# A mixer-and-MLP kernel: the last x load split in two, one DMA transpose of normed tiles done on TensorE, w2's loads side by side

## The chip, the cores and the metric

The kernel runs on one core of one Trainium2 chip. The metric is the device time of one execution in microseconds (us). Before the change the median of three runs is 139.93 us (139.67 to 140.01).

## What is computed

x has 2048 rows of 512; all tensors are bf16. In short:

```python
B, S, D, F = 1, 2048, 512, 1792
h = gelu(layernorm(x) @ w1)                  # w1: 512 x 512
c = D // 4                                   # four groups of 128 columns, shifted along the rows
g0 = h[..., 0*c:1*c] shifted down by 1 row   # zeros come in at the ends
g1 = h[..., 1*c:2*c] shifted up by 1 row
g2 = h[..., 2*c:3*c] shifted down by 2 rows
g3 = h[..., 3*c:   ] shifted up by 2 rows
x1 = x + concat(g0, g1, g2, g3) @ w2         # w2: 512 x 512
out = x1 + gelu(layernorm(x1) @ w3) @ w4     # w3: 512 x 1792, w4: 1792 x 512
```

The layer norm has no gain or bias, and the Gelu is the tanh form.

## The kernel before

**Tiles.** The 2048 rows are 16 tiles of 128. Row `16 p + t` is partition `p` of tile `t`, so a shift by one row is a step from tile `t` to tile `t-1` or `t+1` in the same partition, and only the first and last tiles need a step of one partition. A matmul that wants the 512 features on the partitions needs the tile transposed: four blocks of 128 by 128.

**Two ways through the first layer.** Tiles 0 to 5 are transposed raw by TensorE (`tp0` to `tp5`, line 351) into PSUM banks 6 and 7, copied to `xnT` by ScalarE (`ev`, line 360), multiplied by w1 (`m1r`, line 399), copied out (`rc`, line 409), and the normalisation is made good afterwards on VectorE and ScalarE (`zr`, `g1r`, and a DMA transpose `th_`). Tiles 6 to 15 go in pairs: VectorE takes the statistics (`st0_t`, `ag0_t`, lines 285 and 290), GpSimd the root of two tiles at once (`rs0_t`, line 296), VectorE writes the normed tile into `xn` (`nm0_t`, line 305), one DMA transposes the pair from `xn` to `xnT` (`td0_t`, line 371), TensorE makes h transposed for the pair (`m1p`, line 431: 16 matmuls of 128 by 256), and ScalarE takes the Gelu into `hTf` (`g1p`, line 441, or one tile at a time for tiles 10 and 11, `g1s`, line 446).

**After it.** `m2_t` (lines 457 and 472) multiplies the shifted windows of `hTf` by w2; tiles 8 and 9 are split, so that three of the four products of `m2_8` and two of `m2_9` (`m2_8a`, `m2_9a`) are ahead of those that need tiles 10 and 11. VectorE adds x (`x1_t`, line 482) and makes the second layer norm (`st1`, `ag1`, `nm1`), a DMA transposes the pair (`td1_t`, line 371), and TensorE does the MLP: `m3h` and `m3` (lines 514, 490), Gelu, `m4` (line 533), and VectorE's last add (line 545), with the output DMAs.

**Order.** Each engine runs its operations in an order written out by hand (`firsts`); what is not named follows in the order of the program. The wait of every operation is worked out from what it reads and writes, and an engine, or the DMA queue of SyncE (SP), stands at a waiting operation until it is released: what is queued behind it waits too. SP issues nearly all DMAs, loads and transposes alike, so a transpose that waits for its normed pair also holds the loads behind it, and the other way round. Around the change the order is:

- SP: the x tiles one by one (`ldx6` ... `ldx5`), `ldx12` for tiles 12 to 15 in one DMA, then `td0_6 td0_8 ldw20 td0_10 ldw21 ldw22 ldw23 td0_12 td0_14 ldw3a0 ldw3a1 th_0 ...`
- TensorE: `... tp5 m1r4 cs m1r5 m1p6 m1p8 m1p10 m2_8a m2_9a m2_8 m2_9 m1p12 m1p14 m2_10 ...`
- ScalarE: `... rc5 cse g1p6 g1p8 g1s10 g1s11 g1r0 g1r1 g1p12 g1p14 ...`
- VectorE: `... st0_10 st0_11 nm0_8 nm0_9 ag0_10 ag0_11 st0_12 st0_13 nm0_10 nm0_11 ag0_12 ag0_13 st0_14 st0_15 nm0_12 nm0_13 ag0_14 ag0_15 st0_1 ag0_0 ag0_1 nm0_14 nm0_15 zr0 zr1 st0_2 st0_3 ag0_2 ag0_3 x1_8 x1_9 ...`

The helper `tp(t, n, b, raw)` can transpose `n` tiles into one bank and can read `xn` in place of `x_sb`; before the change it is only called with one raw tile.

Of the kernel before, what the change touches and what calls it, by code (L numbers as in the profile page):

```python
# [26 lines left out]
class Program:  # L27
# [7 lines left out]
    def add(self, eng, name, fn, reads=(), writes=(), dma=False):  # L35
        self.ops.append(Op(name, eng, fn, reads, writes, dma))
# [129 lines left out]
def bass_standalone__mixer_s_mlp__prompt_kernel(nc: bass.Bass, x, w1, w2, w3, w4, out):  # L166
# [15 lines left out]
    with ExitStack() as es:  # L182
# [63 lines left out]
        def bres(b, n, tag):  # L246
            return [(("ps", b + i), tag) for i in range(n)]
# [19 lines left out]
        def load_x(t, n, eng="sp"):  # L267
            add(eng, f"ldx{t}", lambda e: e.dma_start(x_sb[:, t : t + n, :], xd[:, t : t + n, :]),  # L268
                writes=[(("x", i), 0) for i in range(t, t + n)], dma=True)
# [9 lines left out]
        def dst_of(layer, t):  # L279
            return (xn, t, ("xn", t), 0) if layer == 0 else (x1n, POS[t] % 8, ("x1n", POS[t] % 8), t)  # L280
# [61 lines left out]
        def tp(t, n, b, raw):  # L342
            src = x_sb if raw else xn
            rd = [(("x", i), 0) if raw else (("xn", i), 0) for i in range(t, t + n)]

            def f(e):
                ins = None
                for i in range(n):
                    for c in range(DC):
                        o = 1024 * b + (i * DC + c) * P  # L350
                        ins = e.transpose(psb[:, o : o + P], src[:, t + i, P * c : P * (c + 1)], ident[:])  # L351
                return ins

            add("pe", f"tp{t}", f, reads=rd + [("ident", 1)], writes=bres(b, 1, f"tp{t}"))

        def ev(t, n, b, eng="act"):
            src = psb[:, 1024 * b : 1024 * b + n * D]
            dst = xnT[:, t : t + n, :, :].rearrange("p t c s -> p (t c s)")
            if eng == "act":
                f = lambda e: e.activation(dst, src, ACT_F.Copy)  # L360
            else:
                f = lambda e: e.tensor_copy(dst, src)
            add(eng, f"ev{t}", f, reads=bres(b, 1, f"tp{t}"), writes=[(("xT", i), 0) for i in range(t, t + n)])


        def tdma(layer, t, n):
            dst = xnT if layer == 0 else x1nT
            src, k = dst_of(layer, t)[:2]
            p0 = t if layer == 0 else POS[t]
            add("sp", f"td{layer}_{t}",  # L370
                lambda e: e.dma_start(dst[:, p0 : p0 + n, :, :].rearrange("p t c s -> p (t c) s"),
                                      src[:, k : k + n, :].rearrange("p t d -> p (t d)"), transpose=True),
                reads=[dst_of(layer, i)[2:] for i in range(t, t + n)],
                writes=[(("xT", i) if layer == 0 else ("x1T", i), 0) for i in range(t, t + n)], dma=True)
# [205 lines left out]
        load_w1(2, "act")  # L580
        load_w1(3, "sp")
        load_x(1, 1, "act")
        for t, n in ((6, 1), (7, 1), (2, 1), (8, 1), (9, 1), (3, 1), (10, 1), (4, 1), (11, 1), (5, 1), (12, 4)):
            load_x(t, n)
        for c in range(DC):
            load_w2(c)
# [25 lines left out]
            else:  # L612
                norm(0, t)
        for t in range(R, NT, 2):
            tdma(0, t, 2)
        for t, b in ((6, 2), (8, 4), (10, 0), (12, 2), (14, 4)):
            m1p(t, b)
            if t == 10:
# [26 lines left out]
        for t in (8, 10):  # L645
# [8 lines left out]

        firsts = {}
        firsts["pe"] = """wu tp0 cs0 cs1 m1r01 m1r02 tp1 m1r03 m1r0 cs2 m1r12 tp2 m1r1 tp3 m1r2 tp4 m1r3 tp5 m1r4 cs m1r5 m1p6
            m1p8 m1p10 m2_8a m2_9a m2_8 m2_9 m1p12 m1p14 m2_10 m2_11 m2_12 m2_13 m2_14 m2_15""".split()
        firsts["act"] = """ldw10 ldw12 ldx1 table ev0 ev1 ev2 rc0 ev3 rc1 ev4 rc2 ev5 rc3 rc4 rc5 cse g1p6 g1p8 g1s10 g1s11
            g1r0 g1r1 g1p12 g1p14 g2h_0_0_0 g2h_0_0_4 g1r2 g1r3 g2h_0_0_8 g2h_0_0_12 g1r4 g1r5""".split()
        firsts["dve"] = """pada padb padc padd pade padf st0_0 st0_6 st0_7 ag0_6 ag0_7  # L660
            st0_8 st0_9 nm0_6 nm0_7 ag0_8 ag0_9 st0_10 st0_11 nm0_8 nm0_9 ag0_10 ag0_11
# [4 lines left out]
            st1_12 st1_13 ag1_12 ag1_13""".split()  # L666
        firsts["pool"] = """ident0 ident1 neghalf stz ste rs0_6 rs0_8 rs0_10
            rs0_12 rs0_14 rs0_0 rs0_2 rs1_8 rs1_10""".split()
        firsts["sp"] = """ldx0 ldw11 ldw13 ldx6 ldx7 ldx2 ldx8 ldx9 ldx3 ldx10 ldx4 ldx11 ldx5 ldx12 td0_6 td0_8 ldw20 td0_10 ldw21 ldw22 ldw23 td0_12 td0_14
            ldw3a0 ldw3a1 th_0 ldw3a2 ldw3a3 td1_8 ldw3b0 ldw3b1 ldw3b2 ldw3b3 td1_10 th_2 th_4 td1_12 td1_14 ldw4""".split()  # L670

        slots = [4, 0, 2]
# [110 lines left out]
```

## Time and profile before

| | |
|---|---|
| runs | 139.67, 139.93, 140.01 us |
| the profiled execution | 139.81 us, of which its span (first to last instruction) 137.9 |
| granted TensorE clock | 1.000 |
| TensorE busy (matmul) | 131.8 us, 96% of the span |
| VectorE, ScalarE, GpSimd busy | 57.9, 45.6, 12.4 us |
| DMA | 13.23 MB in 25336 packets, of which 17776 under 512 B |

How to read it: the views are of one profiled execution, with times in us from the start of its span. PE is TensorE's matmuls, PEld its weight loads, DVE is VectorE, ACT ScalarE, POOL GpSimd, SP SyncE, and a name with a q is an engine's queue that issues DMAs. A timeline row has the start, the duration, the engine, the line, what is written and read, how many instructions it merges, and in brackets the idle time before it with what ended it. A row of DMA issues ends with the size and the time from issue to landing. The chain is the work that ended last, followed back from the end.

### The profile page before, as it was taken

How to read it: one execution, taken by the hardware profiler on the slowest of the kernel's cores; microseconds unless marked ns; L12 is line 12 of the kernel's file. 1: busy time of each engine (PE TensorE's matmuls, PEld its weight loads, DVE VectorE, ACT ScalarE, POOL GpSimd, SP SyncE). 2: the span in 40 equal slices, each digit the busy share in tenths (PEclk: the TensorE clock that was granted, in tenths of full speed). 3: DMA queues.
4: the chain of work that ended last, by engine and by line, in shares of the span. 5: the costliest groups of instructions: out<-in, count | busy, mean ns of one | idle time of the engine just before them, and what ended most of it. 6: DMA issues, size and time to landing. Idle time of an engine off the chain costs nothing.

```text
span 137.9 us, 1822 instructions
## 1 busy us (share of the span) xinstructions
PE 131.8 (96%) x721; PEld 68.2 (49%) x721; DVE 57.9 (42%) x135; ACT 45.6 (33%) x56; POOL 12.4 (9%) x25
## 2 busy tenths in 40 slices
PE   7897949999999999999999999999999999999993
PEld 2343846748887334444444444444444444444452
DVE  0496995589974787772223000022300002232222
ACT  3478326502896005553000455400045540000000
POOL 2042322220322002222000000000000000000000
DMA  4989979997047792445311100011110001111121
GB/s 115 321 265 212 80 183 234 245 220 186 5 90 138 176 363 70 81 80 103 85 38 38 38 0 5 0 38 38 38 38 0 5 0 38 38 38 38 38 72 47
DMA packets 25336, 13.23 MB, mean 96 GB/s; under 512 B 17776, under 2 KB 24688, under 8 KB 25328
## 3 DMA queue, kind: packets, MB, share of 16 engines
q1 hardware_dynamic: 24752, 12.69, 38.3%
q10 hardware_dynamic: 576, 0.43, 1.2%
q8 instruction: 6, 0.10, 0.3%
q14 instruction: 2, 0.02, 0.0%
HBM read 6.82 MB, written 2.10 MB: 65 GB/s over the span
## 4 chain that ended last, share of the span: by engine, by line
PE 85%; DMA 7%; SPq 4%; DVE 1%; issue 1%
PE ps L533 35%; PE ps L490 26%; PE ps L457 9%; PE ps L514 9%; DMA x_sb<-in_x_dram 4%; PE ps L431 4%; SPq L268 3%; DMA xnT<-xn 3%; PE ps L472 1%; SPq L564 1%; DVE st L285 1%; DVE xn L305 0%; DVE o_sb L545 0%; DVE mv L290 0%
## 5 line engine op out<-in xcount | busy, mean ns | idle before, releaser
L533 PE MATMUL ps<-w_sb,h2T 128*128 128x512 bf16 (+2 forms) x238 | 48.9, 366 | 0.0
L501 ACT ACTIVATE h2T<-ps 128x1024 bf16<-128x1024 f32 x21 | 21.5, 1024 | 46.5 <-PE ps L490 46.5
L545 DVE TENSOR_TENSOR o_sb<-ps,x_sb 128x512 bf16<-128x512 f32 (+2 forms) x17 | 11.2, 660 | 60.9 <-PE ps L533 60.9
L490 PE MATMUL ps<-x1nT,w_sb 128*128 128x512 bf16 x168 | 36.8, 379 | 0.0
L533 PEld LDWEIGHTS ps<-w_sb,h2T 128*128 128x128 bf16 x238 | 22.8, 98 | 25.9
L490 PEld LDWEIGHTS ps<-x1nT,w_sb 128*128 128x128 bf16 x168 | 16.4, 98 | 19.9
L285 DVE BATCH_NORM_STATS2 st<-x_sb 128x6 f32<-128x512 bf16 x32 | 20.4, 678 | 5.2 <-DMA x_sb<-in_x_dram 5.2
L296 POOL TENSOR_TENSOR rstd<-mv,neghalf 128x2 f32<-128x2 f32 x16 | 11.5, 720 | 49.8 <-DVE mv L290 49.6
L457 PE MATMUL ps<-w_sb,hTf 128*128 128x512 bf16 x56 | 12.7, 380 | 0.0
L482 DVE TENSOR_TENSOR x_sb<-ps,x_sb 128x512 bf16<-128x512 f32 x16 | 10.7, 687 | 4.7 <-PE ps L457 3.1
L514 PE MATMUL ps<-x1nT,w_sb 128*128 128x256 bf16 x112 | 12.4, 273 | 0.0
L514 PEld LDWEIGHTS ps<-x1nT,w_sb 128*128 128x128 bf16 x112 | 11.0, 98 | 1.5
L431 PE MATMUL ps<-xnT,w_sb 128*128 128x256 bf16 x80 | 9.2, 273 | 2.6 <-DMA xnT<-xn 2.6
L431 PEld LDWEIGHTS ps<-xnT,w_sb 128*128 128x128 bf16 x80 | 7.6, 98 | 4.4 <-DMA xnT<-xn 3.3
L525 ACT ACTIVATE h2T<-ps 128x1024 bf16<-128x1024 f32 (+1 forms) x8 | 7.1, 915 | 7.7 <-PE ps L514 7.7
L305 DVE TENSOR_SCALAR x1n<-x_sb,mv,rstd 128x512 bf16<-128x512 bf16 x16 | 5.9, 410 | 6.4 <-POOL rstd L296 6.4
L457 PEld LDWEIGHTS ps<-w_sb,hTf 128*128 128x128 bf16 x56 | 5.0, 98 | 7.0 <-DVE x_sb L482 2.2
L399 PE MATMUL ps<-w_sb,xnT 128*128 128x512 bf16 x24 | 6.8, 380 | 0.2
L441 ACT ACTIVATE hTf<-ps 128x1024 bf16<-128x1024 f32 x4 | 4.1, 1024 | 4.3 <-PE ps L431 4.3
L290 DVE BATCH_NORM_AGGREGATE mv<-st 128x2 f32<-128x9 f32 x32 | 4.8, 183 | 0.0
L360 ACT ACTIVATE xnT<-ps 128x512 bf16<-128x512 bf16 x6 | 3.6, 599 | 3.0 <-PE ps L351 3.0
L414 DVE SCALAR_TENSOR_TENSOR zraw<-ncs,mv,yraw 128x512 f32<-128x512 f32 x6 | 4.2, 743 | 0.0
(26 smaller groups left out, 30.5 us busy)
## 6 DMA issues: line engine op xcount, KB each, us to landing
out_dram<-o_sb SPq DMA_DIRECT2D x15, 128.0 KB, 1.8
w_sb<-in_w_dram SPq DMA_DIRECT2D x1, 1792.0 KB, 8.2
x_sb<-in_x_dram SPq DMA_DIRECT2D x11, 128.0 KB, 3.6
w_sb<-in_w_dram SPq DMA_DIRECT2D x4, 256.0 KB, 3.2
w_sb<-in_w_dram SPq DMA_DIRECT2D x6, 128.0 KB, 3.2
w_sb<-in_w_dram SPq DMA_DIRECT2D x4, 192.0 KB, 3.3
x_sb<-in_x_dram SPq DMA_DIRECT2D x1, 512.0 KB, 5.5
w_sb<-in_w_dram ACTq DMA_DIRECT2D x2, 128.0 KB, 3.5
```

The source lines that it names most:

```text
L285: add("dve", f"st{layer}_{t}", lambda e: e.bn_stats(st9[:, i, 0:6], src[:, t, :]), reads=[(r, 0)], writes=[(("st6", i), 0)])
L296: lambda e: e.tensor_tensor(rstd[:, i : i + n], mv[:, i : i + n, 1], neghalf[:, 0:n], ALU.pow),
L399: ins = e.matmul(bank(b), xnT[:, t, c, :], w1_sb[:, c, :], start=(c == 0), stop=(c == DC - 1))
L431: ins = e.matmul(dst, w1_sb[:, c, P * fc : P * (fc + 1)], xnT[:, t : t + 2, c, :], start=(c == 0), stop=(c == DC - 1))
L457: ins = e.matmul(bank(b), hTf[:, c0 : c0 + P], w2_sb[:, j, :], start=(j == 0), stop=(j == DC - 1))
L482: lambda e: e.tensor_tensor(x1_sb[:, t, :], bank(b), x_sb[:, t, :], ALU.add),
L490: ins = e.matmul(bank(b), w3_sb[:, c, P * fc : P * (fc + 1)], x1nT[:, 4 * q : 4 * q + 4, c, :], start=(c == 0), stop=(c == DC - 1))
L501: lambda e: e.activation(h2T[:, fc : fc + 2, q % 2, :], src, ACT_F.Gelu_apprx_tanh),
L514: ins = e.matmul(dst, w3_sb[:, c, P * (fc + i) : P * (fc + i + 1)], x1nT[:, t : t + 2, c, :], start=(c == 0), stop=(c == DC - 1))
L525: lambda e: e.activation(h2T[:, fc : fc + n, q % 2, 256 * k : 256 * (k + 1)], src, ACT_F.Gelu_apprx_tanh),
L533: ins = e.matmul(ps[:, 512 * b : 512 * b + c1 - c0], h2T[:, fc, q % 2, P * i : P * (i + 1)], w4_sb[:, fc, c0:c1], start=(fc == 0), stop=(f ...
L545: lambda e: e.tensor_tensor(o_sb[:, k % 4, c0:c1], ps[:, 512 * b : 512 * b + c1 - c0], x1_sb[:, t, c0:c1], ALU.add),
```

## The change

Three things are changed:

1. x tiles 12 to 15 are loaded by two DMAs of two tiles each, `ldx12` in the old place and `ldx14` on SP behind the first DMA transpose, `td0_6`.
2. The normed pair 10 and 11 is no longer transposed by a DMA. TensorE does eight transposes (`tp10`) from `xn` into bank 7 behind `m1p6`, and ScalarE copies them to `xnT` (`ev10`, 128 by 1024) ahead of `g1p6`.
3. The four loads of w2 are issued one after the other behind `td0_8`; `td0_10` no longer stands between the first and the second.

```diff
-        for t, n in ((6, 1), ..., (5, 1), (12, 4)):
+        for t, n in ((6, 1), ..., (5, 1), (12, 2), (14, 2)):
             load_x(t, n)
...
         for t in range(R, NT, 2):
-            tdma(0, t, 2)
+            if t == 10:
+                tp(t, 2, 7, False)
+                ev(t, 2, 7)
+            else:
+                tdma(0, t, 2)
...
         firsts["pe"] = """wu tp0 cs0 cs1 m1r01 m1r02 tp1 m1r03 m1r0 cs2 m1r12 tp2 m1r1 tp3 m1r2 tp4 m1r3 tp5 m1r4 cs m1r5 m1p6
-            m1p8 m1p10 m2_8a m2_9a m2_8 m2_9 m1p12 m1p14 m2_10 m2_11 m2_12 m2_13 m2_14 m2_15""".split()
-        firsts["act"] = """ldw10 ldw12 ldx1 table ev0 ev1 ev2 rc0 ev3 rc1 ev4 rc2 ev5 rc3 rc4 rc5 cse g1p6 g1p8 g1s10 g1s11
+            tp10 m1p8 m1p10 m2_8a m2_9a m2_8 m2_9 m1p12 m1p14 m2_10 m2_11 m2_12 m2_13 m2_14 m2_15""".split()
+        firsts["act"] = """ldw10 ldw12 ldx1 table ev0 ev1 ev2 rc0 ev3 rc1 ev4 rc2 ev5 rc3 rc4 rc5 cse ev10 g1p6 g1p8 g1s10 g1s11
...
-        firsts["sp"] = """ldx0 ldw11 ... ldx5 ldx12 td0_6 td0_8 ldw20 td0_10 ldw21 ldw22 ldw23 td0_12 td0_14
+        firsts["sp"] = """ldx0 ldw11 ... ldx5 ldx12 td0_6 ldx14 td0_8 ldw20 ldw21 ldw22 ldw23 td0_12 td0_14
             ldw3a0 ldw3a1 th_0 ldw3a2 ldw3a3 td1_8 ldw3b0 ldw3b1 ldw3b2 ldw3b3 td1_10 th_2 th_4 td1_12 td1_14 ldw4""".split()
```

More of the change, by code (lines that the diff above doesn't have):

```diff
@@ L582, in bass_standalone__mixer_s_mlp__prompt_kernel @@
         load_x(1, 1, "act")
-        for t, n in ((6, 1), (7, 1), (2, 1), (8, 1), (9, 1), (3, 1), (10, 1), (4, 1), (11, 1), (5, 1), (12, 4)):
+        for t, n in ((6, 1), (7, 1), (2, 1), (8, 1), (9, 1), (3, 1), (10, 1), (4, 1), (11, 1), (5, 1), (12, 2), (14, 2)):
             load_x(t, n)
@@ L668, in bass_standalone__mixer_s_mlp__prompt_kernel @@
             rs0_12 rs0_14 rs0_0 rs0_2 rs1_8 rs1_10""".split()
-        firsts["sp"] = """ldx0 ldw11 ldw13 ldx6 ldx7 ldx2 ldx8 ldx9 ldx3 ldx10 ldx4 ldx11 ldx5 ldx12 td0_6 td0_8 ldw20 td0_10 ldw21 ldw22 ldw23 td0_12 td0_14
+        firsts["sp"] = """ldx0 ldw11 ldw13 ldx6 ldx7 ldx2 ldx8 ldx9 ldx3 ldx10 ldx4 ldx11 ldx5 ldx12 td0_6 ldx14 td0_8 ldw20 ldw21 ldw22 ldw23 td0_12 td0_14
             ldw3a0 ldw3a1 th_0 ldw3a2 ldw3a3 td1_8 ldw3b0 ldw3b1 ldw3b2 ldw3b3 td1_10 th_2 th_4 td1_12 td1_14 ldw4""".split()
```

## The prediction

> **What bounds the kernel now.** I read the page first, then the chain that ended last in order of time, then TensorE's timeline around the only waits that the chain shows.
>
> ```profile
> span 137.9 us, 1822 instructions
> ...
> PE 85%; DMA 7%; SPq 4%; DVE 1%; issue 1%
> ...
> L431 PE MATMUL ps<-xnT,w_sb 128*128 128x256 bf16 x80 | 9.2, 273 | 2.6 <-DMA xnT<-xn 2.6
> ...
> L399 PE MATMUL ps<-w_sb,xnT 128*128 128x512 bf16 x24 | 6.8, 380 | 0.2
> ...
> L360 ACT ACTIVATE xnT<-ps 128x512 bf16<-128x512 bf16 x6 | 3.6, 599 | 3.0 <-PE ps L351 3.0
> ```
>
> ```profile
> 6.40 0.43 SPq L268
> ...
> 6.87 5.51 DMA x_sb<-in_x_dram
> ...
> 14.36 4.66 DMA xnT<-xn
> ...
> 19.06 1.92 PE ps L431 x16
> ...
> 111.36 24.22 PE ps L533 x126
> ```
>
> TensorE is 85% of the chain. The one large thing on the chain that is not TensorE is x tiles 12-15 (one load, 6.87 to 12.38), VectorE behind it, and the third DMA transpose (td0_10, 14.36 to 19.01). From 19.06 to the end the chain is TensorE alone, so any time by which m1p10 starts sooner shortens the kernel one for one, until another wait appears. TensorE's timeline gives the two waits and the pitch of everything around them:
>
> ```profile
> 10.50 0.39 PE L351 MATMUL ps<-ident,x_sb 128*128 128x128 bf16 x4
> 10.73 1.03 PE L399 MATMUL ps<-w_sb,xnT 128*128 128x512 bf16 x4
> ...
> 11.81 1.03 PE L399 MATMUL ps<-w_sb,xnT 128*128 128x512 bf16 x4
> 13.55 3.67 PE L431 MATMUL ps<-xnT,w_sb 128*128 128x256 bf16 x32 [0.72 <-DMA xnT<-xn]
> 19.06 1.92 PE L431 MATMUL ps<-xnT,w_sb 128*128 128x256 bf16 x16 [1.84 <-DMA xnT<-xn]
> 20.82 2.02 PE L472 MATMUL ps<-w_sb,hTf 128*128 128x512 bf16 x8
> ```
>
> Ends are modelled and overlap, so I count starts. m1r5 is the four at 11.81; they take 1.03 and one takes 0.38, a pitch of (1.03-0.38)/3 = 0.217, so m1p6 could start at 12.68 and starts at 13.55: 0.87 lost. m1p6 and m1p8 are 32 at (3.67-0.27)/31 = 0.110; m1p10 could start at 17.06 and starts at 19.06: 2.00 lost. The whole stake is 2.87 us.
>
> **The landings behind these waits.** From issue to landing, one row for each transfer:
>
> ```profile
> x_sb<-in_x_dram SPq DMA_DIRECT2D x1, 128.0 KB, 4.0
> xnT<-xn SPq DMA_TRANSPOSE x1, 4.3
> xnT<-xn SPq DMA_TRANSPOSE x1, 3.8
> w_sb<-in_w_dram SPq DMA_DIRECT2D x1, 128.0 KB, 3.0
> w_sb<-in_w_dram SPq DMA_DIRECT2D x1, 256.0 KB, 3.2
> x1nT<-x1n SPq DMA_TRANSPOSE x1, 3.0
> x1nT<-x1n SPq DMA_TRANSPOSE x1, 4.9
> ```
>
> In this order: ldx5, td0_6, td0_12, ldw23, ldw3a0, td1_10 (nothing else moving), td1_0. SP's timeline has their issues:
>
> ```profile
> 9.22 3.21 SPq L371 DMA_TRANSPOSE xnT<-xn  x2
> 11.20 1.23 SPq L371 DMA_TRANSPOSE xnT<-xn  x1
> 15.65 2.87 SPq L568 DMA_DIRECT2D w_sb<-in_w_dram  x3
> 18.56 2.62 SPq L371 DMA_TRANSPOSE xnT<-xn  x2
> 54.73 4.28 SPq L371 DMA_TRANSPOSE x1nT<-x1n  x2
> ```
>
> ldx5, issued just ahead of ldx12 at 6.40, lands at 10.4; ldx12 1.98 later. td0_6 is issued at 9.22 and lands at 13.52, 1.14 behind ldx12: it queues behind the load. td0_10 needs 4.66 where a transpose with nothing beside it needs 3.0. What hit it is in the queues of two short windows, 15.56 to 15.58 and 57.40 to 57.43:
>
> ```profile
> q8 instruction: 1, 0.02, 508.8%
> q8 instruction: 1, 0.02, 183.1%
> ```
>
> Each is one 16 KB instruction fetch that starts there. The first lies on td0_10, the second on td1_0 (54.73+4.9 = 59.6, 1.9 late). A fetch lengthens a transpose in flight by 1.7 to 1.9 us. Here the Trainium skill (Runtime: NRT & Kernel Launch, Instruction fetch mechanics) says that crossing such a boundary is mostly hidden; this trace disagrees, with 4.66 against 3.0, and by the page's word the two rivals with a fetch below would have no chance.
>
> **The change, part by part.**
>
> *x in two loads.* ldx12 carries 256 KB in place of 512. Half of 1.98 behind ldx5 is 11.4 (bounds: 10.4 were it free, 12.38 were the bytes not what counts; the halving is the nearest reading as the loads ahead move at about the same rate). td0_6 follows 1.14 later: 12.54; its floor is 9.22+3.0 = 12.2. That is before 12.68, so m1p6's wait goes: **gain 0.87**. ldx14 passes td0_6 on SP and so waits for nm0_7 with it; it is issued at about 10.5, holds SP 0.43, and is done before td0_8's own wait ends at 11.20. Its landing behind a transpose is bounded by ldw3a0, the same size: 3.2 after issue, 13.7. VectorE:
>
> ```profile
> 11.08 0.26 DVE L290 BATCH_NORM_AGGREGATE mv<-st 128x2 f32<-128x9 f32 x2
> 12.40 1.29 DVE L285 BATCH_NORM_STATS2 st<-x_sb 128x6 f32<-128x512 bf16 x2 [1.06 <-DMA x_sb<-in_x_dram]
> 13.61 0.72 DVE L305 TENSOR_SCALAR xn<-x_sb,mv,rstd 128x512 bf16<-128x512 bf16 x2
> 14.42 1.24 DVE L285 BATCH_NORM_STATS2 st<-x_sb 128x6 f32<-128x512 bf16 x2
> 15.58 0.72 DVE L305 TENSOR_SCALAR xn<-x_sb,mv,rstd 128x512 bf16<-128x512 bf16 x2
> 20.45 0.31 DVE L290 BATCH_NORM_AGGREGATE mv<-st 128x2 f32<-128x9 f32 x2
> ...
> 22.31 1.29 DVE L482 TENSOR_TENSOR x_sb<-ps,x_sb 128x512 bf16<-128x512 f32 x2 [1.55 <-PE ps L472]
> ```
>
> It is free at 11.34, so its row runs 1.0 earlier; st0_14 is reached at 13.4 and may wait 0.3 for ldx14. The block that ended at 20.76 ends at 19.8 to 20.0, and nm0_11 at 13.3.
>
> *td0_10 becomes tp10 and ev10.* The DMA leaves SP and the DMA queue. TensorE gets eight transposes between m1p6 and m1p8. Of the same kind the trace has 24:
>
> ```profile
> L351 PE MATMUL ps<-ident,x_sb 128*128 128x128 bf16 x24 | 2.3, 220 | 0.1
> ```
>
> One takes 0.22, but four take 0.39, so they are 0.057 apart, and the matmul behind four that start at 10.50 starts at 10.73; eight cost **0.46** (bounds: this, and 1.76 in series). tp10 starts at 12.68+1.75 = 14.43; nm0_11 is done even at its old 14.33, so m1p8, queued behind tp10, gets no new wait from VectorE. The Trainium skill (TensorE: Matmul & The Clock Gate, Part 4) gives about 275 ns for a transpose in a kernel's context; by that estimate eight cost 2.2 and the gain shrinks to 0.7. The rows agree on the duration (220 ns) and not that it is paid each time, as they overlap.
>
> ev10 is a 1024-wide copy, not in the trace: between the 1.02 that this engine takes for a 1024-wide Gelu (row below) and twice 0.599. I take 1.02, as one copy of twice the width pays the fixed part once.
>
> ```profile
> 15.51 1.02 ACT L441 ACTIVATE hTf<-ps 128x1024 bf16<-128x1024 f32 x1 [1.55 <-PE ps L431]
> ```
>
> tp10's result stands at 15.06, ev10 ends at 16.1, and m1p10 asks for it at 14.89+1.75 = 16.64: covered by m1p8 with 0.5. Queued behind ev10 are g1p6 (to 17.15) and g1p8 (to 18.2); m2_8a waits for both at 18.4, 0.2 spare, nothing left if ev10 takes 1.20. So the wait of m1p10 goes: **gain 2.00**.
>
> *td0_8.* It is now behind ldx14. A transpose behind a copy: ldw23 (the last of the three whose issues end at 18.52, so issued about 18.1; landed at 21.1) and td0_12 (18.56+3.8 = 22.3) are 1.2 apart, so 13.7+1.2 = 14.9; the floor is 11.20+3.0 = 14.2. m1p8 asks at 14.89. It fits, but this is the tightest place: whatever td0_8 is late beyond that is paid one for one.
>
> *w2 together.* ldw21-23 pass the place of td0_10, so they no longer wait for nm0_11. Issued from 12.4 to 14.4, landing 3.0 later by 17.4; m2_8a asks at 18.4. td0_12 is then held by nm0_13 (16.30, now about 15.6) in place of SP's queue, and lands 3.8 later at 19.4; m1p12 follows the eight of m2, at 20.82+8*0.217-2.41 = 20.15. This part costs and gains nothing; its cover is 0.7 us.
>
> *Later.* x1_8 and all behind it up to td1_8, and the w3 loads that SP issues between, hang on TensorE's own m2_8 and move with it, as long as VectorE is free by then: x1_8 started at 22.31, so at 19.9 now, and VectorE is done at 19.8 to 20.0.
>
> **Sum.** 0.87 + 2.00 - 0.46 = 2.41. The profiled execution took 139.81 (span 137.9 and 1.9 around it): 137.40. The median of the three runs is 0.12 above it, so 137.5.
>
> **The rivals.**
>
> *Caught tail.* I take the 16 KB fetches to be TensorE's, the engine with by far the most instructions; the first then falls at a fixed place of its program, the third matmul of m1p8 (which starts at 15.30). With 16 instructions put in ahead, that place is inside tp10, at about 14.6, when td0_8 is due at 14.2 to 14.9. td1_0 was caught 0.3 before it was due and landed 2.2 after the fetch began: td0_8 at 16.8, m1p10 at 18.59, gain 0.47, 139.3 or 139.45 by the median. For: the times meet. Against: the nearer td0_8 is to its floor, the safer.
>
> *Caught in the middle, slower.* If td0_8's packets are mostly still to move at the fetch, it is td0_10 again: that one landed 19.01-15.57 = 3.44 after the fetch began, so 18.04, m1p8 there, m1p10 at 19.8 instead of 19.06: slower by 0.75, 140.6. It decides from a landing of 19.06-1.75 = 17.3 on. For: ldx14 now stands between two transposes that ran back to back. Against: td0_8 would have to be about 1 us later than the rows say.
>
> *The half load brings nothing.* If ldx12 lands at 12.38 because of the queue and not its bytes, td0_6 stays at 13.52: gain 2.00-0.46 = 1.54, 138.3. For: the last 128 KB loads already take 4.0.
>
> *Transposes in series.* Eight at 220 ns, one after the other, are 1.76: gain 1.11, 138.7. Against: the rows of four. The Trainium skill's Part 4, named above, points this way.
>
> **How the numbers follow.** Forecast 0.50; caught tail 0.24; half load 0.10; series 0.03; slower 0.13. A measurement of this kernel tells some 0.3% (0.42 us) from no change. The first, third and fourth are all faster, and a bit over half of the caught tails, whose 139.45 lies beside the line of 139.5: 0.76 faster, 0.11 the same, 0.13 slower. Range: down to 137.1 (the forecast with the spread of the three runs, 0.34), up to 139.5, which takes in the caught tail and leaves out the slower case.
>
> **What would show it.** Right: no wait ahead of m1p6 and m1p10, VectorE without the 1.06 at st0_12, eight L351 matmuls in about 0.6 between m1p6 and m1p8, m1p10 at about 16.6, m2_8a at about 18.4. Wrong: a wait of L431 on the DMA transpose behind tp10 (td0_8, with the fetch inside its flight), a wait of L472 on ScalarE, or of m1p12 on td0_12.

## The result, and the profile after

The changed kernel takes 137.79 us (median of six, 137.44 to 138.75) against 139.80 (139.62 to 140.01): a ratio of 0.9865, 95% interval 0.9832 to 0.9898. That is 2.0 us faster, inside the range and 0.3 above the predicted 137.5. The profiled execution took 137.87, 1.94 less than the one before.

The page of the changed kernel, span and chain:

```profile
span 135.8 us, 1839 instructions
...
PE 98%; issue 0%; DVE 0%
```

The load of x and the DMA transpose are gone from the chain, which is TensorE from 0.77 on. Its timeline (start, duration, engine, line, tiles, count):

```profile
12.24 1.03 PE L399 MATMUL ps<-w_sb,xnT 128*128 128x512 bf16 x4
13.10 1.91 PE L431 MATMUL ps<-xnT,w_sb 128*128 128x256 bf16 x16
14.85 0.61 PE L351 MATMUL ps<-ident,xn 128*128 128x128 bf16 x8
15.30 3.66 PE L431 MATMUL ps<-xnT,w_sb 128*128 128x256 bf16 x32
18.79 2.02 PE L472 MATMUL ps<-w_sb,hTf 128*128 128x512 bf16 x8
20.65 3.66 PE L431 MATMUL ps<-xnT,w_sb 128*128 128x256 bf16 x32
```

No bracket is left in this stretch: both waits are gone. tp10 moves m1p8 from 14.85 to 15.30, 0.45. m1p10 starts at 15.30+1.755 = 17.06 instead of 19.06, 2.00 sooner, and the end moved by 1.94. But m1r5 starts at 12.24 instead of 11.81, and this 0.43 is already there before the change can act. It is in TensorE's first rows; first the kernel before, then the changed one:

```profile
4.24 0.91 PE L387 MATMUL ps<-w_sb,const-bfloat16-1.0 128*128 128x512 bf16 x2
5.09 0.84 PE L399 MATMUL ps<-w_sb,xnT 128*128 128x512 bf16 x2
```

```profile
4.14 0.63 PE L387 MATMUL ps<-w_sb,const-bfloat16-1.0 128*128 128x512 bf16 x1
...
5.30 1.06 PE L399 MATMUL ps<-w_sb,xnT 128*128 128x512 bf16 x2
...
7.25 0.38 PE L387 MATMUL ps<-w_sb,const-bfloat16-1.0 128*128 128x512 bf16 x1
```

The same matmul takes 0.63 at 4.14 and 0.38 at 7.25. In the profile before, TensorE was at full speed by 4.2; here only towards 6. The durations alone show this: the granted clock reads 1.00 in every window of the first 8 us of both profiles, as here in the changed kernel (third figure from the end):

```profile
4.00:5.00 1.00, 0.85 (x6) 0.28 (x3) 0.35 (x1) 0.60 (x1) 0.00 (x0) 1.00 1.04 354
```

The Trainium skill (TensorE: Matmul & The Clock Gate, What's actually happening) says that the clock is released by an activity window that does not start with the kernel, so that the moment changes from run to run. The traces agree that the moment changes, from before 4.2 to between 6.4 and 6.8 by the durations; the window itself is in none of them. The prediction had taken one profile's 11.81 as given.

The landings in the changed kernel, from issue: ldx12 (issued at 6.86), td0_6 (9.23), ldx14 (10.62), td0_8 (11.24), ldw23 (14.14), td0_12 (15.91):

```profile
x_sb<-in_x_dram SPq DMA_DIRECT2D x1, 256.0 KB, 3.5
xnT<-xn SPq DMA_TRANSPOSE x1, 3.2
x_sb<-in_x_dram SPq DMA_DIRECT2D x1, 256.0 KB, 3.3
xnT<-xn SPq DMA_TRANSPOSE x1, 3.7
w_sb<-in_w_dram SPq DMA_DIRECT2D x1, 128.0 KB, 2.7
xnT<-xn SPq DMA_TRANSPOSE x1, 3.4
```

td0_8 lands at 14.9, as predicted, 0.36 ahead of m1p8. ScalarE and VectorE behind the new steps:

```profile
15.50 1.02 ACT L360 ACTIVATE xnT<-ps 128x1024 bf16<-128x1024 bf16 x1 [1.11 <-PE ps L351]
16.42 1.94 ACT L441 ACTIVATE hTf<-ps 128x1024 bf16<-128x1024 f32 x2
```

```profile
13.96 1.29 DVE L285 BATCH_NORM_STATS2 st<-x_sb 128x6 f32<-128x512 bf16 x2 [0.64 <-DMA x_sb<-in_x_dram]
```

ev10 takes the 1.02 that was assumed, and g1p8 ends at 18.36, 0.43 ahead of m2_8a. st0_14 now waits 0.64 for ldx14, off the path.

### The profile page after: what moved, and what is told of

The parts are those of the page before. It is cut to its first block, busy times and chain, and to the rows that moved or that the text cites. A ratio compares the mean times of both kernels' runs of the same rounds, so it can differ in the third digit from the quotient of the medians.

```text
span 135.8 us, 1839 instructions
## 1 busy us (share of the span) xinstructions
PE 132.4 (97%) x729; PEld 69.2 (51%) x729; DVE 57.8 (43%) x135; ACT 46.4 (34%) x57; POOL 12.4 (9%) x25
## 4 chain that ended last, share of the span: by engine, by line
PE 98%; issue 0%; DVE 0%
PE ps L533 36%; PE ps L490 27%; PE ps L457 9%; PE ps L514 9%; PE ps L431 6%; PE ps L399 4%; PE ps L556 2%; PE ps L351 1%; PE ps L472 1%; PE ps L387 1%; DVE o_sb L545 0%
## 5 line engine op out<-in xcount | busy, mean ns | idle before, releaser
L490 PEld LDWEIGHTS ps<-x1nT,w_sb 128*128 128x128 bf16 x168 | 16.4, 98 | 19.8
L514 PE MATMUL ps<-x1nT,w_sb 128*128 128x256 bf16 x112 | 12.4, 273 | 0.0
L360 ACT ACTIVATE xnT<-ps 128x512 bf16<-128x512 bf16 (+1 forms) x7 | 4.6, 660 | 4.6 <-PE ps L351 4.6
L441 ACT ACTIVATE hTf<-ps 128x1024 bf16<-128x1024 f32 x4 | 4.0, 1024 | 2.0 <-PE ps L431 2.0
```

What stands on the lines that cost most here:

```text
L490: ins = e.matmul(bank(b), w3_sb[:, c, P * fc : P * (fc + 1)], x1nT[:, 4 * q : 4 * q + 4, c, :], start=(c == 0), stop=(c == DC - 1))
L514: ins = e.matmul(dst, w3_sb[:, c, P * (fc + i) : P * (fc + i + 1)], x1nT[:, t : t + 2, c, :], start=(c == 0), stop=(c == DC - 1))
```

## The experiments

The theory is the prediction's: the gain is the two waits of TensorE less the transposes. Its rivals: one part alone carries it; the place of the loads does; a new wait stands behind.

**The split alone.** `split_only` is the kernel before with:

```diff
-        ... (5, 1), (12, 4)):
+        ... (5, 1), (12, 2), (14, 2)):
-  ... ldx12 td0_6 td0_8 ldw20 td0_10 ldw21 ldw22 ldw23 td0_12 td0_14
+  ... ldx12 td0_6 ldx14 td0_8 ldw20 td0_10 ldw21 ldw22 ldw23 td0_12 td0_14
```

> The kernel before with the x load split (ldx14 behind td0_6), td0_10 still a DMA between ldw20 and ldw21. Theory (the gain is the sum of two waits, less the transposes): the wait of 0.87 ahead of m1p6 goes; nm0_11 ends at 13.2 instead of 14.33, so td0_10 is issued 1.1 us earlier and m1p10 starts when it lands: 13.2+3.0 = 16.2 at best (then TensorE itself sets 16.5 and the gain is 2.4, 137.4 us), 13.2+4.7 = 17.9 if it is as slow as before (gain 1.2, 138.6). Rival (the transposes on TensorE are what pays): td0_10 stays late by the same DMA traffic, m1p10 not before 18.5, gain under 0.6, 139.2 or more.

138.64 us, ratio 0.9938 (0.9908 to 0.9967): a gain of 0.95 over the kernel before on the same chip. Its TensorE timeline, then the landings of td0_10, ldw21 and ldw22, and the share of the 16 DMA engines that instruction fetches took between 16.0 and 16.5:

```profile
13.39 5.46 PE L431 MATMUL ps<-xnT,w_sb 128*128 128x256 bf16 x48
19.32 1.90 PE L472 MATMUL ps<-w_sb,hTf 128*128 128x512 bf16 x8 [0.47 <-DMA w_sb<-in_w_dram]
```

```profile
xnT<-xn SPq DMA_TRANSPOSE x1, 3.5
w_sb<-in_w_dram SPq DMA_DIRECT2D x1, 128.0 KB, 4.0
w_sb<-in_w_dram SPq DMA_DIRECT2D x1, 128.0 KB, 3.7
q8 instruction: 1, 0.02, 15.5%
```

The 48 matmuls of m1p6, m1p8 and m1p10 run through: the DMA transpose is in time once VectorE is earlier, and m1p10 starts at about 16.9, inside the theory's 16.2 to 17.9. The time is a little outside its range, as the least gain was to be 1.2, and the wait turns up elsewhere: w2's loads stand behind td0_10 and have the fetch in their flight, and m2_8a waits for them. ldw22, the last that it reads, is issued at 15.34 and lands at 19.0.

**The transposes alone.** `tp_only` is the changed kernel with x tiles 12 to 15 in one load again.

```diff
-        ... (12, 2), (14, 2)):
+        ... (12, 4)):
-  ... ldx12 td0_6 ldx14 td0_8 ldw20 ...
+  ... ldx12 td0_6 td0_8 ldw20 ...
```

> The changed kernel with x tiles 12-15 still in one load ahead of td0_6; td0_10 is gone, tp10 and ev10 are in, w2's parts together. Theory: m1p6 keeps its wait for td0_6 (starts at 13.55), tp10 at 15.30, m1p8 at 15.76, m1p10 at 17.5 instead of 19.06: gain 1.54, 138.3 us. Rival (the split carries it, by way of an earlier VectorE): nm0_11 late, tp10 waits and m1p10 is not before 18.5: gain under 0.6.

137.95 us, ratio 0.989 (0.9861 to 0.9919): a gain of 1.64, where 1.54 was expected. Run again beside the changed kernel:

> tp10 and ev10 without the split of the x load, on the same chip as the changed kernel. Theory: it keeps the wait ahead of m1p6, so it starts m1p6 at 13.5 to 14.1 whatever the early clock does; slower than the changed kernel by 0.2 to 0.8 us, and with less spread. Rival (the split is worth nothing, the transposes are all): the same time within 0.1.

> The changed kernel again, beside the kernel with the transposes alone. Theory: no wait on TensorE from the first x tile on, so what is left of the spread is the moment at which the granted clock comes to full speed in the first stage (seen at 4.0 to 6.8 us in the traces so far, which put m1p6 anywhere from 12.7 to 13.4): 137.2 to 138.2 us, profile by profile 139.81 - 2.41 + the lateness of m1p6 behind 12.68. Rival (the 0.4 that the changed kernel fell short of its sum is a new wait): a wait on TensorE of about 0.4 shows behind 13 us.

138.08 (137.96 to 138.29) and 138.03 (137.41 to 138.32): the same within 0.1, so the rival is right that the split adds almost nothing on top. Why is in the two timelines, `tp_again` first (with an early wait for an x tile), then `after_again`, with td0_8 of the latter (issued at 11.75):

```profile
6.19 0.40 PE L351 MATMUL ps<-ident,x_sb 128*128 128x128 bf16 x4 [0.55 <-DMA x_sb<-in_x_dram]
...
13.54 1.92 PE L431 MATMUL ps<-xnT,w_sb 128*128 128x256 bf16 x16 [0.36 <-DMA xnT<-xn]
15.29 0.61 PE L351 MATMUL ps<-ident,xn 128*128 128x128 bf16 x8
15.74 3.66 PE L431 MATMUL ps<-xnT,w_sb 128*128 128x256 bf16 x32
```

```profile
13.12 1.91 PE L431 MATMUL ps<-xnT,w_sb 128*128 128x256 bf16 x16
14.87 0.61 PE L351 MATMUL ps<-ident,xn 128*128 128x128 bf16 x8
15.69 3.65 PE L431 MATMUL ps<-xnT,w_sb 128*128 128x256 bf16 x32 [0.21 <-PE ps L351]
```

```profile
xnT<-xn SPq DMA_TRANSPOSE x1, 3.8
```

With the split, m1p6 starts 0.42 sooner, and m1p8 then stands until td0_8 lands at 15.6 behind ldx14: 15.69 against 15.74. This is the wait of about 0.4 that the rival in `after_again` named. The bracket names TensorE, which had long been done; tp10 would have let m1p8 start at 15.32, and td0_8 is the other thing it waits for. A third run of the changed kernel:

> The changed kernel as it is, for comparison on the same chip: 137.8 to 138.1 us. Theory: its profile shows either no wait on TensorE behind 13 us or one ahead of m1p8, as long as td0_8 is late, and the time follows the start of m1p10 (139.81 at 19.06, 137.87 at 17.06).

137.97, with m1p8 at 15.31 and no wait. The two cases of the expectation are the two that were seen. Against the kernel before on their own chips the two later runs of the changed kernel gain 1.66 and 1.69, less than the 2.0 of the first, and the two of `tp_only` 1.64 and 1.61.

**w2's place alone.** `w2_only` is the kernel before with:

```diff
-  ... td0_6 td0_8 ldw20 td0_10 ldw21 ldw22 ldw23 td0_12 ...
+  ... td0_6 td0_8 ldw20 ldw21 ldw22 ldw23 td0_10 td0_12 ...
```

> The kernel before with nothing but the order of SP changed: the four loads of w2 directly behind td0_8, td0_10 behind them. Theory: w2's place gains nothing by itself; td0_10 is issued at about 14.4 as before, now queues behind 512 KB, and lands at 18.2 (3.8, as td0_12 behind w2 did) to 19.5: 139.0 to 140.3. Rival (the place among the loads is what delayed td0_10): it lands 3.0 after issue, at 17.4, and m1p10 gains 1.6: 138.2.

Slower, with a ratio of 1.0082 (1.0036 to 1.0128). Its ten runs fall into two groups of five, 139.8 to 140.3 and 141.8 to 142.5, and the median of all, 141.02, lies between the two. The lower group has a granted clock of 1.000 and a median of 140.15, inside the expected 139.0 to 140.3; the upper one has 0.987 or 0.988 in each run. The profiled one (141.79) shows what the upper group pays. TensorE's row of m1p10, then three windows of 1 us (busy time and count of PE, PEld, DVE, ACT, POOL, then the granted clock, the DMA share and GB/s):

```profile
19.49 3.30 PE L431 MATMUL ps<-xnT,w_sb 128*128 128x256 bf16 x16 [2.32 <-DMA xnT<-xn]
```

```profile
18.00:19.00 1.00, 0.00 (x0) 0.00 (x0) 1.00 (x3) 0.23 (x1) 0.00 (x0) 1.00 0.76 163
20.00:21.00 1.00, 1.00 (x7) 0.73 (x5) 0.19 (x2) 0.00 (x0) 0.69 (x1) 0.50 1.23 231
24.00:25.00 1.00, 1.00 (x8) 0.51 (x7) 0.58 (x1) 1.00 (x2) 0.00 (x0) 1.00 0.00 0
```

td0_10 lands at 14.93+4.5 = 19.4, and after a wait of 2.32 the granted clock is 0.50 for some 3 us (it reads 0.92 from 19 to 20, so the fall comes with m1p10 already running): m1p10 takes 3.30 instead of 1.92. w2 together is no gain in itself; once td0_10 has left SP, its loads stand together anyway.

**Without transposes on TensorE.** `split_td10_first` has the split, and td0_10 as a DMA ahead of all of w2.

```diff
-  ... ldx12 td0_6 td0_8 ldw20 td0_10 ldw21 ldw22 ldw23 td0_12 ...
+  ... ldx12 td0_6 ldx14 td0_8 td0_10 ldw20 ldw21 ldw22 ldw23 td0_12 ...
```

> The split load, no transposes on TensorE, td0_10 directly behind td0_8 and all of w2 behind it. Theory: td0_10 is issued at 13.2 and lands at 16.3 to 16.9, m1p10 starts at about 16.6 to 17.0, without the 0.46 of the transposes; w2's parts are issued from 14.5 to 16.3 and land by 19.3, m2_8a wants them at 18.4 and may wait up to 0.6. Together 137.2 to 138.0, level with the changed kernel. Rival (a transposition by DMA of this pair always lands late): m1p10 at 18.5 or later, 139.2 or more.

139.26, ratio 0.9974 (0.995 to 0.9997), a miss. m1p10 starts at 15.27+1.755 = 17.0 as the theory said, so the rival's late transpose is not the reason, though its time is met. m2_8a starts only at 20.23:

```profile
15.27 3.65 PE L431 MATMUL ps<-xnT,w_sb 128*128 128x256 bf16 x32 [0.47 <-PE ps L431]
20.23 1.91 PE L472 MATMUL ps<-w_sb,hTf 128*128 128x512 bf16 x8 [1.31 <-ACT hTf L446]
```

m2_8a needs nothing of L446, which the bracket names; it needs ldw22, issued at 15.79, which landed 4.2 later, at 19.99, with a fetch at 17.4 inside its flight. The 0.47 ahead of m1p8 is td0_8 behind ldx14 again (11.49+3.7 = 15.2). A DMA transpose of this pair can be in time, but in both orders tried here w2 then is not.

**Who has slack.** Four idle matmuls ahead of m1p6, in both kernels.

```diff
+        warmup("wx", 4, 5)
-  ... cs m1r5 m1p6 ...
+  ... cs m1r5 wx m1p6 ...
```

> The kernel before with four idle matmuls (128 by 512, into a free bank; 4 x 0.217 = 0.87 us of TensorE time) between m1r5 and m1p6. Theory: there TensorE has 2.87 us of waits to give, so the added work hides: the same time within 0.2. Rival (the start of m1p6 carries through to the end in this kernel too): 0.4 to 0.9 slower.

> The changed kernel with the same four matmuls at the same place. Theory: nothing on TensorE waits any more, so all of it is paid: 0.87 us slower than the changed kernel (0.7 to 0.9). Rival (another chain, by way of VectorE or the DMAs, sets m1p10 as well): less than half of it is paid.

The kernel before hides them: 139.54, ratio 0.9989 (0.996 to 1.0018). In its profile m1p6 starts 0.78 later than in the profile before and m1p10 no later, with 0.97 of wait left:

```profile
13.46 1.03 PE L556 MATMUL ps<-const-bfloat16-1.0 128*128 128x512 bf16 x4
14.33 3.65 PE L431 MATMUL ps<-xnT,w_sb 128*128 128x256 bf16 x32
18.96 1.92 PE L431 MATMUL ps<-xnT,w_sb 128*128 128x256 bf16 x16 [0.97 <-DMA xnT<-xn]
```

The changed kernel goes from 138.03 to 138.55: 0.52 of the 0.87, below the 0.7 to 0.9 expected. The rest, 0.35, is about the wait for td0_8 (0.37 in `after_again`): the added work runs inside it. The profiles say the same: m1p8 starts at 16.33 against 15.69, which is 0.87 and 0.14 of a later m1r5 less 0.37, and the profiled times are 0.65 apart.

**Where the fetch falls.** `before_pad32` puts 16 more matmuls, each with its weight load, ahead of all others: 32 more TensorE instructions.

```diff
-  ins = e.matmul(bank(b), ones, ones_wide, start=True, stop=True)
+  ins = e.matmul(ps[:, 512 * b : 512 * b + 156], ones, ones_wide[:, 0:156], start=True, stop=True)
...
-  warmup("wu", 7, 5)
+  warmup("wu", 23, 5)
```

> The kernel before with its warm-up as 23 matmuls of 156 columns in place of 7 of 512: the same columns, but 32 TensorE instructions more ahead of everything else. Theory (the 16 KB instruction fetch makes td0_10 late, and comes at a place of TensorE's program): the fetch comes 1.5 to 1.8 us earlier, at about 13.9, and td0_10 lands 3.0 to 3.4 after its issue, at 17.5: 138.2 to 138.5 us, or 138.9 if it catches td0_8 instead. Rival (the fetch only coincides, td0_10 is slow by itself behind the load of w2): it lands 4.4 to 4.7 after its issue again, 139.6 us.

139.60, ratio 0.9995 (0.9977 to 1.0013). The fetch lies between 15.4 and 15.6 again, not 1.6 earlier, and td0_10 is as late as before:

```profile
q8 instruction: 1, 0.02, 45.2%
xnT<-xn SPq DMA_TRANSPOSE x1, 4.5
```

So the fetch does not follow the count of TensorE's instructions as the prediction had it. The three traces of the changed kernel show the same: the fetch begins at 16.1, 17.0 and 16.5, which is 0.8, 1.3 and 1.2 behind the start of m1p8. What sets its moment stays open, and as it did not move here, this run does not separate its cost from td0_10's own.

**Two attempts at more.** `td8_first` takes td0_8 back ahead of ldx14, with VectorE's row arranged around the later tiles.

```diff
-  sp:   ... td0_6 ldx14 td0_8 ldw20 ...
+  sp:   ... td0_6 td0_8 ldx14 ldw20 ...
-  dve:  ag0_13 st0_14 st0_15 nm0_12 nm0_13 ag0_14 ag0_15 st0_1 ag0_0 ag0_1 nm0_14 nm0_15 zr0 zr1
+  dve:  ag0_13 st0_1 ag0_0 ag0_1 nm0_12 nm0_13 zr0 st0_14 st0_15 ag0_14 ag0_15 zr1 nm0_14 nm0_15
-  pool: rs0_12 rs0_14 rs0_0
+  pool: rs0_12 rs0_0 rs0_14
```

> The changed kernel with td0_8 ahead of ldx14 on SP again, and VectorE's row put so that it does not stand at st0_14 for it: st0_1, ag0_0, ag0_1, nm0_12, nm0_13 and zr0 go ahead of st0_14, zr1 behind ag0_15 (GpSimd's rs0_0 ahead of rs0_14). Theory (in the changed kernel td0_8 behind ldx14 has become the wait of about 0.35 ahead of m1p8): td0_8 lands by 14.7 instead of 14.9 to 15.6, m1p8 starts right behind tp10, and the time is 0.2 to 0.4 us below the changed kernel. Rival (nothing is left to win there, the early clock sets the rest): the same time within 0.1, or slower by up to 0.5 where td0_14, now normed 2 us later, reaches m1p14 late.

138.75 against 137.97 for the changed kernel on the same chip: slower by 0.78, more than the rival's 0.5 and by another way. m1p8 does start right behind tp10, but the w2 loads are now behind ldx14, and ldw22 (issued at 15.26, with a fetch at 17.4 in its flight) takes 4.8; m2_8a waits again. The profiled run, 139.16, is the longest of the six, and m1p6 was already 0.65 later in it than in the changed kernel:

```profile
15.95 3.66 PE L431 MATMUL ps<-xnT,w_sb 128*128 128x256 bf16 x32
20.41 1.69 PE L472 MATMUL ps<-w_sb,hTf 128*128 128x512 bf16 x7 [0.80 <-ACT hTf L446]
```

```profile
w_sb<-in_w_dram SPq DMA_DIRECT2D x1, 128.0 KB, 4.8
```

`tp10_in_wait` has both x loads ahead of td0_6 and tp10 inside TensorE's wait for it.

```diff
-  sp:  ... ldx12 td0_6 ldx14 td0_8 ...
+  sp:  ... ldx12 ldx14 td0_6 td0_8 ...
-  pe:  ... m1r5 m1p6 tp10 m1p8 ...
+  pe:  ... m1r5 tp10 m1p6 m1p8 ...
```

> The changed kernel with both x loads ahead of td0_6 (ldx12, ldx14, td0_6, td0_8) and tp10 ahead of m1p6 instead of behind it. Theory (the split buys little because td0_8 pays for it; what counts is where TensorE's waits lie): m1p6 waits for td0_6 until about 13.5 again, but tp10 now lies inside that wait (nm0_11 done at about 13.2, tp10 to 13.65), td0_8 is back to back with td0_6 and in time, m1p10 starts at 17.1 to 17.3: 137.8 to 138.0 us, level with the changed kernel and with less spread. Rival (tp10 ahead of m1p6 only delays it, since nm0_11 comes late): m1p6 at 14 or later, 138.3 or more.

138.28, ratio 0.9909 (0.9874 to 0.9944): the rival's case, with nm0_11 too late and m1p6 at 14.05. TensorE's row, and ldx12's landing:

```profile
13.59 0.62 PE L351 MATMUL ps<-ident,xn 128*128 128x128 bf16 x8 [0.82 <-DVE xn L305]
```

```profile
x_sb<-in_x_dram SPq DMA_DIRECT2D x1, 256.0 KB, 4.7
```

With ldx14 directly behind it, ldx12 takes 4.7 instead of 3.5, and VectorE's st0_12 is 0.35 later. No version beat the changed kernel, and `tp_only` is level with it.

## Why the prediction was right, and where it was off

- **The wait ahead of m1p10, 2.00, and its price, 0.46:** right. It is gone, and tp10 cost 0.45. `tp_only`, which has these without the split, gained 1.64 and 1.61 where 1.54 was worked out. The case of transposes in series is out: the eight start about 0.056 apart. It is these two terms that carry the gain.
- **The wait ahead of m1p6, 0.87:** the term that was mis-sized. The wait is gone in the changed kernel, so the mechanism holds, but it was worth 0.45 in the profile (13.55 to 13.10) and 0.05 on the medians of the run with and without the split. Two things took it. The step "m1p6 could start at 12.68" read the start of m1r5 off a single profile, in which TensorE was at full speed early and had no wait for an x tile behind that; in others m1p6 could start at 12.6 to 13.8. The later starts have the slow first rows, or a wait of 0.2 to 0.55 for an x tile, or both. `tp_again` has only the wait, the 0.55 of its first row above: it is at full speed by 4.0 and m1r5 still starts at 12.15. In the kernel before such a delay is covered by the waits, as `before_wx4` shows; in the changed one 0.52 of 0.87 was paid in `after_wx4`. Whether it makes the spread of the changed kernel's runs is not shown: the six of the result lie 1.3 us apart and those of the kernel before beside them within 0.4, but with the later experiments the runs of the kernel before lie 1.1 to 2.7 apart. And td0_8, "the tightest place", is late by up to 0.37 as it stands behind ldx14. That the first median came within 0.3 of the forecast is partly luck: the later gains of 1.66 and 1.69 are 0.7 short of the 2.41 of the sum.
- **The half load brings something:** ldx12 landed at 10.4, sooner than the 11.4 of halving, and td0_6 at 12.4, predicted 12.5. That rival is out as a mechanism, though its time, 138.3, is nearer to the 138.0 of the changed kernel's later runs than the forecast is.
- **The landings of td0_8 and td0_12, and how long ev10 takes:** within 0.1 of the forecast. w2 landed at 16.8 where 17.4 was said. VectorE is less well met: st0_14 waited 0.64 where 0.3 was said, and the block ended at 20.35 where 19.8 to 20.0 was said. This cost nothing, as x1_8 starts 1.50 behind m2_8a, against 1.49 in the kernel before.
- **The caught transposes:** not seen in the changed kernel. The step that put the fetch at 14.6, at a fixed place of TensorE's program, failed: it was at 16.1 there, and did not move for 32 instructions. What remains is that each of these late transfers had a fetch inside its flight: td0_10 (4.7, 4.5, 4.5) or the w2 loads (4.0, 4.2, 4.8). The reverse does not hold. In the changed kernel ldw23 was in flight at the fetch and landed 2.7 after its issue, at 16.84, and td0_12, issued just before it, took 3.4 and had 1.3 to spare (15.91+3.4 = 19.3, against m1p12 at 20.65). So the 1.7 to 1.9 that the prediction put down to a fetch is not shown to be its price.

## What to carry to other kernels

When the engine on the path has waits, a delay ahead of them is covered as long as it is shorter; once they go, what was covered (here a slow first stage and a transpose behind a load) is paid, and the last wait removed is worth less than it measures. Price a removed wait from several profiles of its start, not from one. Where loads and transposes share a queue, moving one moves the wait to the next: three reorderings here put it on w2.

## What the runs showed of the hardware

- With the same warm-up, TensorE's matmuls came to full speed anywhere from before 4.2 us to between 6.4 and 6.8 (`split_only`), with the granted clock of the profile at 1.00; the traces with no other delay ahead have m1r5 at 11.8 to 12.5.
- Behind a wait of 2.32 us in `w2_only` the granted clock fell to 0.50 for about 3 us; behind the wait of 1.84 in the profile before it did not. All five runs of `w2_only` over 141 us have a granted clock of 0.987 or 0.988, and so have three of the kernel before on other chips (141.1 to 141.3).
- Eight 128 by 128 transposes cost 0.45 us of TensorE's time at a mean duration of 0.22 each.
- A 256 KB load of x (ldx12) landed 3.5 us after its issue in the changed kernel, with no other x load issued behind it for 3.8 us, and 4.7 in `tp10_in_wait`, with another directly behind it.
